# A cached-attention decode block on one core: TensorE's tail moved 820 instructions on, one load cut by rows, one by columns

## The chip, the cores and the metric

One core of one Trainium2 chip. The metric is the device time of one execution in microseconds (us); several runs are taken and their median counts. The profile is of one more execution, whose own time stands beside its span.

## What is computed

A decode step of a transformer block, batch 2, one new position, model width 448, all in fp32:

```python
h  = x + _A_ref(_layernorm(x), k_cache, v_cache, wq, wo)   # 16 heads of 256, 8192 cached keys
h2 = h + _B_ref(_layernorm(h), w_gate, w_up, w_down)       # ((h Wg) * (h Wu)) Wd, width 1792
```

`_A_ref` projects q, takes scores against the cached keys (scaled by 256^-0.5), a softmax over the 8192 keys, mixes the cached values and projects by wo. Keys and values are 2 x 16 x 8192 x 256 floats each: of the 561 MB that are read, 537 MB are these two caches.

## The kernel before

The work is 32 attention items, one for each head and batch row (`NQ = H * B`), and then the output projection and the gated feed-forward layer. Keys of item i, [128 partitions, 64 positions, 256], land in one of two buffers `k0`, `k1`; values in the one buffer `v`. VectorE multiplies the keys by the spread query (L436) and sums over the 256 (L445), all in place; TensorE and ScalarE make the softmax from the scores, and TensorE mixes the values (`mix`, L527). Once the last keys are used, weights take the place of keys and values: wo in `k0`; gate and up in `k1`; down in `v`.

**Queues.** All loads but x's are issued by SyncE (SP), in the order of the list that `load` (L175) builds, each by one `dma_start` (its line in the profile is L176). At the end of that list come wo, the last values in two parts, gate's weights (L283), up's weights in three loads by columns (L284, `wu0` to `wu2`: 3584, 1792 and 896 columns), and down's weights in six (L287, `DOWN`: 4, 4, 2, 2, 1 and 1 of the 14 chunks of 448 columns). Up's loads have no wait of their own; down's wait for the last mix, `("M", NQ - 1)`. Every load has 128 rows, one a partition. x's load (L259) has two rows and is issued by ScalarE. Gate, up and down are packed on the host so that a partition's share of a load is one contiguous row.

**Engines.** `Engine.do` adds an instruction with its waits and its mark to a list for each engine; `Engine.emit` (L81) writes the list out when the program is built. `roll` (L59) makes a loop of it: TensorE's 32 turns (`tensor_turn`, L591) are one loop (L627), with parts for the last turn alone (`only`). What stands behind L627 is TensorE's last part: `last_head` (L577), the sums of the second layernorm, `project` for gate and for up (L710; matmuls at L715 and L726), the transposes of the product (L760), and down's matmuls (L779 for the first 8 chunks, L805 for the other six, four column quarters q each). One fp32 matmul is two weight loads and two passes on TensorE, so that counts in the profile are twice those in the code.

**Hints.** Before an engine's list, `emit` writes a branch that is never taken to a block `aside` at the end of the engine's code, and a hint for the target of the branch in `aside` (L90 to L97):

```python
hint = e.mark_branch_hint_location()
e.reg_mov(never, 0)
e.br_lt(never, 0, on_true=name + "aside", on_false=name + "main")
```

**Matmuls that are not read.** `busy(n)` (L534) puts four matmuls of n columns, eight passes, into a bank that nobody reads any more. They stand in the last turn (384), at L631 (256), L633 (320), L748 (384, between gate's and up's projection), L750 (256) and L773 (192).

**The end.** Each of down's matmuls waits for the load of its chunk, `("wd", down_of[k])` (L809). After the last, VectorE copies y out of PSUM (L815) and SP stores it (L818).

## Time and profile before

| | |
|---|---|
| median of 3 runs | 1301.18 us (1301.15 to 1301.63) |
| the profiled execution | 1300.94 us, span 1299.6 us (1.34 us lie outside the span) |
| busy | DVE 1132.5 us (87%), PE 471.1 (36%), PEld 149.9, ACT 83.5, POOL 0.8 |
| DMA | 561.28 MB, 432 GB/s over the span, 11382 packets |
| chain that ended last | DMA 48%, DVE 41%, issue 8%, PE 2% |

A span runs from the first to the last instruction of the program. The busy line tells how long each engine worked at all; the chain tells which work followed on which, back from the end. A DMA share is the mean over the core's 16 DMA engines: 1.00 when all 16 move data throughout a stretch (in a short stretch it can come out above 1, since a packet counts from its start). PE's matmuls are pipelined, so its rows overlap a little.

### The profile page before, as it was taken

How to read it: one execution, taken by the hardware profiler on the slowest of the kernel's cores; microseconds unless marked ns; L12 is line 12 of the kernel's file. 1: busy time of each engine (PE TensorE's matmuls, PEld its weight loads, DVE VectorE, ACT ScalarE, POOL GpSimd, SP SyncE). 2: the span in 40 equal slices, each digit the busy share in tenths (PEclk: the TensorE clock that was granted, in tenths of full speed). 3: DMA queues.
4: the chain of work that ended last, by engine and by line, in shares of the span. 5: the costliest groups of instructions: out<-in, count | busy, mean ns of one | idle time of the engine just before them, and what ended most of it. 6: DMA issues, size and time to landing. Idle time of an engine off the chain costs nothing.

```text
span 1299.6 us, 7381 instructions
## 1 busy us (share of the span) xinstructions
PE 471.1 (36%) x2870; PEld 149.9 (12%) x2870; DVE 1132.5 (87%) x265; ACT 83.5 (6%) x245; POOL 0.8 (0%) x8
## 2 busy tenths in 40 slices
PE   3643214334323433323334322433322343332368
PEld 0111001101001101101101101101100110100113
DVE  1999988889888889888889988889988888988861
ACT  1100000000000000000000000000000000000000
POOL 0000000000000000000000000000000000000000
PEclk9866566666566666556666656666656666655669
DMA  9999999999999999999999999999999999999998
GB/s 412 428 450 422 448 424 444 426 436 436 422 450 422 450 422 448 424 444 426 436 436 422 450 422 450 422 448 424 444 426 436 436 422 450 422 450 422 448 422 365
DMA packets 11382, 561.28 MB, mean 432 GB/s; under 512 B 1394, under 2 KB 1652, under 8 KB 2420
## 3 DMA queue, kind: packets, MB, share of 16 engines
q1 hardware_dynamic: 11376, 561.25, 99.8%
q8 instruction: 2, 0.03, 0.0%
q10 hardware_dynamic: 4, 0.00, 0.0%
HBM read 561.19 MB, written 0.06 MB: 432 GB/s over the span
## 4 chain that ended last, share of the span: by engine, by line
DMA 48%; DVE 41%; issue 8%; PE 2%; SPq 0%; DVEq 0%; ACT 0%
DMA k<-in_A_k_cache_dram 45%; DVE s L445 21%; DVE k L436 19%; DMA v<-in_wq_dram 2%; DMA v<-in_wd_dram 1%; PE bank L376 1%; PE bank L561 1%; PE bank L527 1%; DVE m L458 0%; DVE nm L464 0%; DVE rl L469 0%; SPq L176 0%; PE bank L551 0%; DVEq L149 0%; PE bank L367 0%
## 5 line engine op out<-in xcount | busy, mean ns | idle before, releaser
L436 DVE TENSOR_TENSOR k<-k,qb 128x4096 f32<-128x4096 f32 x64 | 555.3, 8676 | 122.6 <-DMA k<-in_A_k_cache_dram 98.9
L445 DVE TENSOR_REDUCE s<-k 128x16 f32<-128x4096 f32 x64 | 555.2, 8675 | 1.1
L527 PE MATMUL bank<-v,p 128*2 128x512 f32 x2048 | 289.5, 729 | 348.0 <-DMA v<-in_A_v_cache_dram 348.0
L527 PEld LDWEIGHTS bank<-v,p 128*2 128x2 f32 x2048 | 53.2, 96 | 577.2 <-DMA v<-in_A_v_cache_dram 370.7
L597 PE MATMUL bank<-nm,row 1*128 1x1 f32 x64 | 18.6, 357 | 230.9 <-DVE nm L464 230.9
L594 PE MATMUL bank<-ident,m 128*1 128x128 f32 x32 | 11.9, 372 | 179.7 <-DVE m L458 179.7
L502 ACT ACTIVATE o_sb<-bank 128x512 f32<-128x512 f32 x32 | 19.1, 597 | 625.9 <-PE bank L527 625.9
L597 PEld LDWEIGHTS bank<-nm,row 1*128 1x128 f32 x64 | 15.9, 306 | 240.3 <-DVE nm L464 240.3
L619 PE MATMUL bank<-sel,o_sb 128*128 128x1 f32 x256 | 33.7, 253 | 22.6 <-ACT o_sb L502 22.6
L367 PE MATMUL bank<-q_sel,ones 2*128 2x256 f32 x68 | 40.2, 691 | 0.0
L619 PEld LDWEIGHTS bank<-sel,o_sb 128*128 128x128 f32 x256 | 31.0, 191 | 52.3 <-ACT o_sb L502 52.3
L376 PE MATMUL bank<-v,xz 128*2 x64 | 30.5, 639 | 16.3 <-DMA v<-in_wq_dram 16.3
L492 ACT ACTIVATE nb<-bank 128x1 f32<-128x1 f32 x32 | 5.5, 171 | 427.0 <-PE bank L597 427.0
L601 PE MATMUL bank<-lsum,ones 128*128 128x1 f32 x64 | 18.7, 361 | 23.5 <-ACT p L494 23.5
L594 PEld LDWEIGHTS bank<-ident,m 128*1 128x1 f32 x32 | 2.5, 79 | 182.7 <-DVE m L458 182.7
L601 PEld LDWEIGHTS bank<-lsum,ones 128*128 128x128 f32 x64 | 16.0, 309 | 26.2 <-ACT p L494 26.2
L404 ACT ACTIVATE q_sel<-q_all,ident 2x256 f32 (+1 forms) x35 | 17.2, 492 | 0.0
L413 ACT ACTIVATE qb<-bank 128x256 f32<-128x256 f32 x34 | 13.0, 383 | 58.2 <-PE bank L367 58.2
L367 PEld LDWEIGHTS bank<-q_sel,ones 2*128 2x128 f32 x68 | 16.4, 297 | 2.2 <-issue 1.7
L494 ACT ACTIVATE p<-s,nb 128x64 f32<-128x64 f32 x32 | 11.1, 348 | 1.0
L504 ACT ACTIVATE oT<-bank,rl 128x2 f32 x32 | 8.4, 262 | 42.0 <-PE bank L619 42.0
L487 DVE COPY k<-bank 128x448 f32<-128x448 f32 x1 | 0.6, 624 | 11.6 <-PE bank L561 11.6
(89 smaller groups left out, 96.0 us busy)
## 6 DMA issues: line engine op xcount, KB each, us to landing
v<-in_wq_dram SPq DMA_DIRECT2D x1, 7168.0 KB, 19.7
k<-in_wo_dram SPq DMA_DIRECT2D x1, 7168.0 KB, 39.6
k<-in_A_k_cache_dram SPq DMA_DIRECT2D x1, 6144.0 KB, 38.1
v<-in_A_v_cache_dram SPq DMA_DIRECT2D x1, 6144.0 KB, 22.8
k<-in_wg_dram SPq DMA_DIRECT2D x1, 3136.0 KB, 27.8
k<-in_A_k_cache_dram SPq DMA_DIRECT2D x1, 2048.0 KB, 24.1
v<-in_A_v_cache_dram SPq DMA_DIRECT2D x1, 2048.0 KB, 27.3
k<-in_wu_dram SPq DMA_DIRECT2D x1, 1792.0 KB, 31.8
```

Source lines behind the costliest of these rows:

```text
L367: lambda *_: nc.tensor.matmul(qb_ps, ones[:B, :], q_sel, start=True, stop=True),
L376: lambda turn, k=k, c=c, xs=xs, base=base: nc.tensor.matmul(q_ps[k], xz[:, xs, :], wq_t[:, bass.ds(turn * QG + base, QG)], start=(c == 0), ...
L404: return nc.scalar.activation(q_sel, q_sb[:, bass.ds(at, DH)], AF.Copy, scale=ident[:B, b : b + 1])
L413: lambda *_: nc.scalar.activation(qb[i % 2], qb_ps, AF.Copy),
L436: lambda *_: nc.vector.tensor_mul(kt, kt, q[:, None, :].to_broadcast([P, hi - lo, DH])),
L445: lambda *_: nc.vector.tensor_reduce(s[:, lo:hi], kt, axis=AX.X, op=ALU.add),
L502: A.do(lambda *_: nc.scalar.activation(o_sb, o_ps, AF.Copy), ("M", i), done=("osb", i))
L527: lambda *_, t=t, g=g: nc.tensor.matmul(o_ps[g : g + 2, :], p_t[:, 2 * t : 2 * t + 2], v_sb[:, 2 * t : 2 * t + 2, :], start=(t < 4), stop= ...
L594: lambda *_: nc.tensor.transpose(mT_ps, m_t, ident), ("m", i), done=("T", i)
L597: lambda *_: nc.tensor.matmul(nb_ps, row, nm, start=True, stop=True),
L601: lambda *_: nc.tensor.matmul(l_ps, ones, lsum, start=True, stop=True),
L619: lambda *_, c=c, k=k: nc.tensor.matmul(oT_ps[:, c : c + 1], o_sb[:, (2 * k + c) * P : (2 * k + c + 1) * P], sel[:, k : k + 1], start=(k = ...
```

## The change

Four edits. (1) Behind TensorE's loop a branch skips 820 instructions that are never run (1640 waits, two to an instruction) to a block `far`, which holds TensorE's last part; a hint for `far` is given at the start of TensorE's program, and the hint for `aside` is now given at the start of `far`. (2) The first quarter of `wu0` (`F // 2`, 896 columns, which is 3584 bytes a row) is loaded ahead by two loads, of rows 0 to 103 and of rows 104 to 127, onto the semaphore of `wu0`, which now counts 48; the rest of `wu0` (2688 columns) follows. (3) `busy(384)` between the two projections is left out. (4) The last chunk of down's weights comes in two loads of 224 columns each; the matmuls of its last two quarters wait for the second one.

```diff
+APART, EVEN = 820, 104
@@ Engine.__init__
-        self.items, self.ahead, self.gap = [], 0, None
+        self.items, self.ahead, self.gap, self.far, self.apart_by = [], 0, None, None, 0
@@ Engine.emit
         self.emit_ops(self.items[: self.ahead], known, seen)
+        at = self.ahead
+        if self.far is not None:
+            hint = e.mark_branch_hint_location()
+            e.reg_mov(never, 0)
+            self.emit_ops(self.items[at : self.far], known, seen)
+            e.br_lt(never, 0, on_true=name + "unused", on_false=name + "far").branch_hint(hint)
+            with nc.body(name + "unused", valid_engines=here):
+                for _ in range(2 * self.apart_by):
+                    e.wait_ge(self.sems[0], 0)
+                nc.br(name + "far", engines=here)
+            nc.switch_bb(name + "far")
+            at = self.far
         hint = e.mark_branch_hint_location()
...
-            self.emit_ops(self.items[self.ahead : self.gap], known, seen)
+            self.emit_ops(self.items[at : self.gap], known, seen)
@@ decode_block, the loads
-    for k, part in enumerate((slice(0, 2 * F), slice(2 * F, 3 * F), slice(3 * F, NF * D))):
-        load(S, wu_t[:, part], wu[:, part], landing(f"wu{k}"), ("wu", k))
+    wu_ends, s_wu = (2 * F, 3 * F, NF * D), [landing(f"wu{k}") for k in range(3)]
+    for rows in (slice(0, EVEN), slice(EVEN, P)):
+        load(S, wu_t[rows, : F // 2], wu[rows, : F // 2], s_wu[0], "wu_even")
+    for k, part in enumerate(map(slice, (F // 2, *wu_ends), wu_ends)):
+        load(S, wu_t[:, part], wu[:, part], s_wu[k], ("wu", k), n=16 * (3 if k == 0 else 1))
     at = 0
     for k, n in enumerate(DOWN):
-        load(
-            S, v_flat[:, at * D : (at + n) * D], wd[:, at * D : (at + n) * D],
-            landing(f"wd{k}"), ("wd", k), ("M", NQ - 1),
-        )
+        mid = [at * D + 2 * W] if k == len(DOWN) - 1 else []
+        ends = [at * D, *mid, (at + n) * D]
+        for j, cols in enumerate(map(slice, ends, ends[1:])):
+            load(
+                S, v_flat[:, cols], wd[:, cols], landing(f"wd{k + j}"), ("wd", k + j),
+                ("M", NQ - 1),
+            )
         at += n
@@ decode_block, TensorE
     T.roll(0, NQ, 1, tensor_turn)
+    T.far, T.apart_by = len(T.items), APART
...
-    busy(384)
     project(u_ps, wu_t, lambda c: ("wu", max(c - 1, 0)), "u", "u_blank")
...
-                ("hmT_in", j // 2), ("wd", down_of[k]),
+                ("hmT_in", j // 2), ("wd", down_of[k] + (k == NF - 1 and q >= 2)),
```

## Rows read from the trace of the kernel before

**Rows 1.** page, the DMA line of part 2, and part 3 (queue, kind: packets, MB, share)

```profile
DMA  9999999999999999999999999999999999999998
...
q1 hardware_dynamic: 11376, 561.25, 99.8%
q8 instruction: 2, 0.03, 0.0%
q10 hardware_dynamic: 4, 0.00, 0.0%
```

**Rows 2.** chain of work that ended last, in order of time, from 1276 us (start, us, what)

```profile
1276.97 0.33 SPq L176
...
1279.31 17.89 DMA v<-in_wd_dram
...
1297.24 0.44 PE bank L805 x8
...
1297.71 0.27 DVE k L815
```

**Rows 3.** stretches near the end (us, granted TensorE clock, DMA share of 16 engines, GB/s)

```profile
1295.40:1295.80 0.40, 1.00 0.38 143
1295.80:1296.00 0.20, 1.00 0.18 72
1296.05:1296.25 0.20, 1.00 0.12 45
1296.60:1296.85 0.25, 1.00 0.13 50
1296.90:1297.20 0.30, 1.00 0.00 0
```

**Rows 4.** DMA queues, instruction fetch: first 60 to 80 us, then 1282 to 1284.5 us

```profile
q8 instruction: 1, 0.02, 0.3%
...
q8 instruction: 1, 0.02, 2.4%
```

**Rows 5.** DMA queues and issues, 1298 to 1299.6 us (engine, KB each, us to landing)

```profile
q1 hardware_dynamic: 144, 0.06, 12.9%
...
out_dram<-k SPq DMA_DIRECT2D x1, 56.0 KB, 1.5
```

**Rows 6.** page, part 6: two of the loads (KB each, us from issue to landing)

```profile
k<-in_wg_dram SPq DMA_DIRECT2D x1, 3136.0 KB, 27.8
...
k<-in_wu_dram SPq DMA_DIRECT2D x1, 1792.0 KB, 31.8
```

**Rows 7.** timeline (start, us, engine line op tiles shape count [idle before])

```profile
1238.42 8.54 PE L527 MATMUL bank<-v,p 128*2 128x512 f32 x64 [11.61 <-DMA v<-in_A_v_cache_dram]
...
1254.63 1.37 SPq L176 DMA_DIRECT2D k<-in_wu_dram  x3
...
1269.86 7.05 PE L527 MATMUL bank<-v,p 128*2 128x512 f32 x64
...
1277.63 1.05 PE L619 MATMUL bank<-sel,o_sb 128*128 128x1 f32 x8
...
1278.61 0.61 PE L539 MATMUL bank<-k,sel 128*2 128x256 f32 x8
...
1286.82 0.83 PE L539 MATMUL bank<-k,sel 128*2 128x384 f32 x8
...
1287.46 2.74 PE L715 MATMUL bank<-k,xr 128*32 128x512 f32 x24
...
1293.93 0.93 PE L779 MATMUL bank<-v,k 128*2 128x448 f32 x8 [0.23 <-DMA v<-in_wd_dram]
...
1295.15 0.59 PE L805 MATMUL bank<-v,k 128*32 128x112 f32 x16 [0.29 <-DMA v<-in_wd_dram]
...
1297.24 0.40 PE L805 MATMUL bank<-v,k 128*32 128x112 f32 x8 [0.16 <-DMA v<-in_wd_dram]
```

**Rows 8.** a stretch before the last but one item's mix (us, PE busy, granted clock, DMA, GB/s)

```profile
1225.50:1238.00 12.50, 1.32 (x3) 0.50 0.95 410
```

## The prediction

> **What bounds the kernel now.** The page comes first. Its DMA line is at 9 tenths or more in 39 of 40 slices and 8 in the last, and the packets of q1 fill 99.8% of 16 engines' span [rows 1]. 561.25 MB over 0.998 x 16 x 1299.6 us is 27.0 KB per us and engine. The compute engines work beside that: the DMA queue is never empty, so the kernel ends when the last of the 16 engines has worked off its share, plus what follows that.

> The chain in order of time shows what follows. SP issues the last of the down loads at 1279.31, it has landed 17.89 us later, at 1297.20; then 0.44 us of eight matmul passes of L805, the copy (0.27), and the store, 1299.6 being the span's end [rows 2]. So 2.4 us lie behind the last landing.

> Third, the last microseconds in short stretches [rows 3]. The reader is to see steps of 1/16 = 0.0625 in the DMA share: 0.38 on average up to 1295.8, then 0.18 (three engines), 0.12 and 0.13 (two), and 0 from 1296.90. Thirteen engines are done by 1295.8, a third straggler between 1296.00 and 1296.05 (1296.04 in what follows), and two work on alone for 0.9 us. The landing at 1297.20 is 0.30 after their last packet.

> Why two? The other entry that moves bytes is the fetch of instructions, 2 packets in the whole span [rows 1]. One falls between 60 and 80 us and took 0.3% of 16 x 20 us, about 1.0; one between 1282 and 1284.5, 2.4% of 16 x 2.5, or 0.96 us, of one engine [rows 4]. An engine that served one is that much late with its loads, and since its queue never empties it stays late. Two fetches, two engines late by 0.9: I read them as cause and effect, though no row numbers the engines.

> **The change, part by part.**

> [...]

> Cutting rows costs packets: 144 packets of the store took 12.9% of 16 x 1.6 us, 23 ns each, of which 448 bytes are 17 ns, so 6 ns more for each. An engine of the twelve gets 10 more packets here, 8 with the cut down chunk, and three marks: about 0.12 us, a spared engine 0.06.

> *The last down chunk in two loads.* The second half waits alone at the end, so four passes instead of eight stand behind the last landing. The eight took 0.40 [rows 7]; four save 0.2. The added wait delays nothing but the last two quarters of y; the first two run earlier.

> *SP.* Two more issues for up, one more for down, at 1.37/3 = 0.46 us [rows 7]. Up's were issued 31.8 us before the first landed [rows 6], down's last 17.89 before; SP's next work is the store. Nothing at the end; without that cover, 1.4 us.

> *The unread matmuls* (eight passes of 384 columns): 1286.82 to the next start at 1287.46, 0.64 us of TensorE [rows 7]. Up's projection follows at once, since its first load, issued at 1254.63, landed 31.8 later, 1286.4 [rows 6]; at the end it gives nothing, as TensorE waits for down's loads at 1293.93, 1295.15 and 1297.24 [rows 7]. No idle time appears there, so the clock should stay at 1.00 [rows 3].

> *TensorE's jump.* A hint at the program's start lies in the wait for wq. After the last turn come a branch over 820 instructions, a hint and a second branch. The rows don't show such sequencer work. Cover: between L619's start at 1277.63 and the next matmul at 1278.61, 1.0 us [rows 7], the sequencer has only to run ahead. Lower bound 0 (no gain: nothing at this place holds the end); upper bound, if the code isn't there, a fetch of 0.96 behind one row of gate's weights (3136 KB over 128 rows, 24.5 KiB, 0.93 us [rows 6]), 1.9. I take 0, as neither fetch of now leaves a visible stall. The fetches themselves don't go away: each still costs one engine 0.96, and longer code may add one.

> *Sum.* If the late engines are spared ones: 1296.90 - 1.06 + 0.06 = 1295.90, no longer last. The thirteen go to 1295.8 + 0.27 + 0.12 = 1296.2, the third straggler to 1296.04 + 0.39 = 1296.43. That one now sets the end: landing at 1296.73, 0.47 earlier; with 0.2 from the four passes, 0.67. The profiled execution took 1300.94 (span 1299.6 and 1.34 around it), 0.24 under the median of 1301.18. I predict 1301.18 - 0.67 = 1300.5.

> **Rivals.**

> A, relief misses: a late engine is one of the twelve. 1296.90 + 0.39 = 1297.29, then 0.2 saved: +0.2, 1301.4; where the late engine is the one that neither gains nor loses, about 1301.1. For it: three of 16 are spared and no row names them. Against: the fetches, never on one engine twice here, seem to take engines in turn, and three spared neighbours cover a turn of up to three.

> B, more relief: the third straggler is spared as well, the end falls to 1296.2, 1300.3.

> C, the loads spread over all 16: -0.2 alone and a few marks, 1301.0. The hint doing nothing belongs to D.

> D, slower: the jump finds its code missing. Place: the branch after the last turn. Price: 1.9 less a cover of 0 to 1.0, so TensorE's tail is 0.9 to 1.9 late. [...] It decides beyond TensorE's slack: 0.64 of unread matmuls and idle 0.23, 0.29 and 0.16 [rows 7], 1.3 against the present end, 0.6 against the forecast. Alone: 1300.8 to 1301.8; with the clock, up to 1303.3; a second missing block, 1.9 more, 1304 to 1305. For it: two fetches in 1300 us show that the code isn't all loaded ahead [rows 1, 4]; against: the hint, given long before, and that neither fetch of now held TensorE, whose clock stays at 1.00 behind the second [rows 3].

> [...]

> **How the numbers follow.** 0.2% of 1301.18 is 2.6 us, about what a measurement of this kernel can tell from no change; all cases but D's far end lie inside. Chances: forecast 0.5, B 0.1, A 0.17, C 0.05, D up to 1301.8 0.08, D beyond 0.07 (past 2.6 us 0.03), unforeseen gain 0.03. The range holds the first five less their edges: from B with 0.4 of run-to-run spread, 1299.9, to A and D's near end, 1301.8. The forecast's own range, with 0.2 of spread and the marks, is 1300.2 to 1300.8. Faster by over 0.2%: 0.01, as no term reaches 2.6; slower 0.03; same 0.96.

> **What would show it.** Right: q1 near 11376 + 117 + 36 + 144 = 11673 packets (11680 if all loads had 16 marks); the DMA share drops to zero at about 1296.4 with no pair working on alone; the last landing at 1296.7; four passes of L805 behind it; L539 gone from before up's projection; no gap between L619 and the next matmul. Wrong: a pair alone to 1297.2 (A), the steps of now unchanged (C), a gap of over a microsecond behind L619 or a clock under 1.00 after 1278 (D), or more than three fetch packets on the engines.

## The result, and the profile after

The changed kernel takes 1303.76 us (median of 22 runs, 1301.62 to 1304.40), the kernel before, run beside it, 1301.18 (1300.96 to 1301.73). The ratio is 1.0018, with a 95% interval of 1.0012 to 1.0023: 2.6 us slower, where 1300.5 was predicted, in a range up to 1301.8. The profiled execution took 1303.55 us (span 1302.2), 2.61 more than that of before.

The page after, the lines that answer to [rows 1]:

```profile
DMA  9999999999999999999999999999999999999998
...
q1 hardware_dynamic: 11673, 561.25, 99.7%
q8 instruction: 2, 0.03, 0.0%
q10 hardware_dynamic: 4, 0.00, 0.0%
```

Same bytes, and 11673 packets as forecast, which fits 104 rows on 13 engines and 24 on 12 (117 and 36 packets with the end marks). The queue is as full as before, and there are still two instruction fetches. The chain after, in order of time (start, us, what), against [rows 2]:

```profile
1278.39 20.25 DMA v<-in_wd_dram
1298.64 0.04 issue
1298.68 1.56 PE bank L829 x32
1300.25 0.02 issue
1300.27 0.28 DVE k L839
```

The load still holds the end. The chain puts all 32 passes of L829 into one piece; the last four of them waited once more, for the last load, which landed at 1299.79:

```profile
1299.84 0.14 PEld L829 LDWEIGHTS bank<-v,k 128*32 128x32 f32 x4 [0.17 <-DMA v<-in_wd_dram]
```

y's copy (L839) starts at 1300.27, not 1297.71: 2.56 later. So the loss is all ahead of it. TensorE's timeline after (start, us, engine line operation, idle before and its releaser in brackets):

```profile
1277.73 1.05 PE L643 MATMUL bank<-sel,o_sb 128*128 128x1 f32 x8
...
1278.71 0.61 PE L563 MATMUL bank<-k,sel 128*2 128x256 f32 x8
...
1283.76 1.91 PE L740 MATMUL bank<-k,xr 128*32 128x512 f32 x16 [0.87 <-DMA k<-in_wg_dram]
...
1289.04 1.91 PE L740 MATMUL bank<-k,xr 128*32 128x512 f32 x16 [1.07 <-DMA k<-in_wu_dram]
...
1296.51 0.93 PE L803 MATMUL bank<-v,k 128*2 128x448 f32 x8 [0.71 <-DMA v<-in_wd_dram]
```

The jump lies between L643 and L563: 0.98 from start to start, as in [rows 7]. The first new wait is for gate's weights, behind which the cut quarter of up lies in the queue; before, gate's matmuls started without one:

```profile
1282.68 1.91 PE L715 MATMUL bank<-k,xr 128*32 128x512 f32 x16
```

So the next view is the DMA's rate while that quarter is loaded (us, granted TensorE clock, DMA share, GB/s), first before, then after:

```profile
1280.20:1280.70 0.50, 1.00 0.95 402
...
1280.80:1283.20 2.40, 1.00 1.04 441
1283.20:1286.20 3.00, 1.00 0.96 401
```

```profile
1280.20:1280.70 0.50, 1.00 0.71 287
1280.70:1281.20 0.50, 1.00 1.35 351
1281.20:1281.70 0.50, 1.00 0.98 244
1281.70:1282.20 0.50, 1.00 1.14 237
1282.20:1282.70 0.50, 1.00 1.37 272
...
1280.80:1283.20 2.40, 1.00 1.06 242
1283.20:1286.20 3.00, 1.00 1.00 370
```

This is the reading that counts: the share stays at 1, but 242 GB/s are moved in place of 441. The engines are as busy, their packets take longer. From 1280.8 to 1286.2 that is 2.4 x 199 + 3.0 x 31 = 571 KB less, 1.3 us at 432 GB/s. And at the very end, against [rows 3]:

```profile
1297.20:1297.50 0.30, 1.00 0.28 99
1297.70:1298.30 0.60, 1.00 0.13 48
1298.50:1299.40 0.90, 1.00 0.07 24
```

Two engines still work on alone, and then one (0.07) by itself up to 1299.49. To see what became of that one I followed single packets of the trace, each one starting where the last one on its engine ended. A last gate row (25088 bytes) and what came behind it, on the engine that ends last:

```
                      last gate row       then, until the first 3584 columns of up are in
kernel before   931 ns, ends 1281.755     8 rows of 14336 bytes, end 1286.01: 4.26 us
kernel after   1733 ns, ends 1282.676     8 rows, mark, 2 rows of 3584 bytes, mark,
                                          8 rows of 10752 bytes, end 1288.55: 5.88 us
```

So this engine had 8 + 2 rows: it is one of the twelve, not one of the three that were spared. Those ten packets of 3584 bytes took 141 to 348 ns, 237 in the mean; down's packets of that size, later in the same trace, took 140. It lost 0.92 us in the gate row's end and 1.62 behind it, 2.54 in all; the last landing came 2.59 later (1299.79 for 1297.20).

### The profile page after: what moved, and what is told of

It is laid out like the page before. It is cut to its first block, busy times and chain, and to the rows that moved or that the text cites. A ratio compares the mean times of both kernels' runs of the same rounds, so it can differ in the third digit from the quotient of the medians.

```text
span 1302.2 us, 7371 instructions
## 1 busy us (share of the span) xinstructions
PE 472.4 (36%) x2862; PEld 149.6 (11%) x2862; DVE 1132.5 (87%) x265; ACT 83.5 (6%) x245; POOL 0.8 (0%) x8
## 3 DMA queue, kind: packets, MB, share of 16 engines
q1 hardware_dynamic: 11673, 561.25, 99.7%
## 4 chain that ended last, share of the span: by engine, by line
DMA 74%; PE 25%; issue 0%; SPq 0%; DVE 0%
DMA v<-in_A_v_cache_dram 71%; PE bank L551 23%; PE bank L400 2%; DMA v<-in_wd_dram 2%; DMA v<-in_wq_dram 2%; PE bank L829 0%; SPq L193 0%; PE bank L391 0%; DVE k L839 0%
## 5 line engine op out<-in xcount | busy, mean ns | idle before, releaser
L643 PE MATMUL bank<-sel,o_sb 128*128 128x1 f32 x256 | 33.7, 253 | 22.6 <-ACT o_sb L526 22.6
L643 PEld LDWEIGHTS bank<-sel,o_sb 128*128 128x128 f32 x256 | 31.0, 191 | 52.3 <-ACT o_sb L526 52.3
```

The lines of the kernel that those rows point to most:

```text
L643: lambda *_, c=c, k=k: nc.tensor.matmul(oT_ps[:, c : c + 1], o_sb[:, (2 * k + c) * P : (2 * k + c + 1) * P], sel[:, k : k + 1], start=(k = ...
```

## The experiments

Each was run in turn with the kernel before. The letters in the expectations: T, the load by rows is slow in itself (P: because of the partitions that its engines write at one time); J, the jump costs; Q, the number of loads in the queue; U, the unequal shares of rows; R, the number and size of row loads, whichever rows they hold; F, the fetches go with the length of the code.

**Without the cut by rows, and the cut alone.** The first is the changed kernel with up's loads as before, the second the kernel before with edit 2 alone.

```diff
-    wu_ends, s_wu = (2 * F, 3 * F, NF * D), [landing(f"wu{k}") for k in range(3)]
-    for rows in (slice(0, EVEN), slice(EVEN, P)):
-        load(S, wu_t[rows, : F // 2], wu[rows, : F // 2], s_wu[0], "wu_even")
...
+    for k, part in enumerate((slice(0, 2 * F), slice(2 * F, 3 * F), slice(3 * F, NF * D))):
+        load(S, wu_t[:, part], wu[:, part], landing(f"wu{k}"), ("wu", k))
```

> The changed kernel with wu0 loaded in one load of 128 rows as before; the jump, the missing unread matmuls and the down chunk in two loads stay. Theory T: the two loads of 104 and 24 rows make engines write to the same group of SBUF partitions and halve the rate while they run (changed kernel: 244, 237 and 272 GB/s in half microseconds from 1281.2 to 1282.7, where before had 430 to 459), which costs every engine over 1 us. Then all of the loss goes: 1301.0, 0.2 under before by the four passes, and 430 GB/s in that stretch. Rival J: the jump over 820 instructions (with the later fetch of code) is the loss: stays at 1303.7. Rival Q: the longer list of loads on SP (the last load was issued 5 us late, at 1284.58) is the loss: half back at most, 1302.5, since one more load than before is left.

> The kernel before with only the first quarter of wu0 as 104 and 24 rows. T: slower by the whole loss and by the four passes that the changed kernel saves, 1303.9, with the same dip to some 240 GB/s. J: 1301.2, no loss. Q: two more loads than before against three in the changed kernel, about 1302.9.

Without the cut: 1301.27 us, ratio 0.9999 (0.9990 to 1.0008). The cut alone: 1303.71, ratio 1.0016 (1.0007 to 1.0025). The whole loss is edit 2; the other three together are worth nothing that shows. The same two stretches, without the cut, and with the cut alone:

```profile
1280.80:1283.20 2.40, 1.00 0.98 412
1283.20:1286.20 3.00, 1.00 0.99 418
```

```profile
1280.80:1283.20 2.40, 1.00 1.13 261
1283.20:1286.20 3.00, 1.00 0.96 346
```

The dip goes with the cut, and J falls. In the second trace the engine that ends last shows the same two things: its last gate row took 1616 ns, and 8 + 2 rows of 3584 bytes follow. The first also has edit 4, whose end shows in its timeline:

```profile
1297.63 0.14 PEld L826 LDWEIGHTS bank<-v,k 128*32 128x32 f32 x4 [0.16 <-DMA v<-in_wd_dram]
1298.06 0.27 DVE L836 COPY k<-bank 128x112 f32<-128x112 f32 x1 [2.12 <-PE bank L826]
```

The four passes behind the last landing start at 1297.63, and the copy 0.43 later; before, with eight passes, 0.47 [rows 2]. So half as many of them save 0.04, not 0.2.

**The quarter whole, and cut at 64.** The changed kernel with the quarter ahead in one load of 128 rows; and with `EVEN = 64`, where both halves run on all 16 engines (q1 has 11680 packets, 80 for each half) and none is spared. In the runs with another number of loads the count of `wu0`'s semaphore follows that number.

```diff
-    for rows in (slice(0, EVEN), slice(EVEN, P)):
+    for rows in (slice(0, P),):
...
```

> The changed kernel with the first quarter of wu0 in one load of 128 rows, ahead of the rest: the columns are still cut, the rows are not. T: no dip, 1301.0 to 1301.1 (eight more packets of 6 ns an engine). Q or a cost of short rows (3584 bytes): one load fewer than in the changed kernel, 1302.5 to 1303. J: 1303.7.

> The changed kernel with the quarter cut at row 64 instead of 104: two loads of 64 rows, 64 being divisible by 16, so that no engine is spared and each has 4 rows of either. [...] Rival U: the loss comes from sparing three engines (they run ahead and out of step) or from two more rows on the twelve others: no dip, 1301.1.

Whole: 1301.57, ratio 1.0001 (0.9992 to 1.0010). Cut at 64: 1303.04, ratio 1.0013 (1.0004 to 1.0022). In the same order:

```profile
1280.80:1283.20 2.40, 1.00 1.06 431
```

```profile
1280.80:1283.20 2.40, 1.00 1.06 277
1283.20:1286.20 3.00, 1.00 0.99 370
```

So a smaller load ahead, of rows as short as those of the cut, costs nothing that the interval can tell. Q falls: this kernel issues as many loads as the one with the cut alone, which took 2.1 us more. And a cut that gives all engines equal shares still loses 1.7 of the 2.6 us, so U is not the main cause; it may hold a part of the rest. T's sizes were off: the whole quarter came out 0.3 us above no change, which its interval can't tell from it, and the cut at 64 cost 1.5 on top, where half the rate for its 448 KB would cost 1.06 (an estimate, 448 KiB / 432 GB/s).

**Same sizes, other rows.** Three loads of 64, 32 and 32 rows, first with rows 32 to 95 as the 64, then with rows 0 to 63.

```diff
-    for rows in (slice(0, EVEN), slice(EVEN, P)):
+    for rows in (slice(32, 96), slice(0, 32), slice(96, P)):
...
```

```diff
-    for rows in (slice(0, EVEN), slice(EVEN, P)):
+    for rows in (slice(0, 64), slice(64, 96), slice(96, P)):
...
```

> The changed kernel with the quarter in three loads: rows 32 to 95 (64 rows), then 0 to 31, then 96 to 127. [...] Loss 0.5 us against the same without a row cut, 1301.6 plus 0.3, 1301.9, against the kernel of the next run, with the same sizes, 0.5 less; no dip in its first half microsecond. Rival R: any cut by rows costs alike (short loads, rows out of step): as the next run.

> The changed kernel with the quarter in three loads of the same sizes but rows 0 to 63, 64 to 95, 96 to 127. [...] R: no difference between the two.

Rows 32 to 95: 1301.78, ratio 1.0003 (0.9994 to 1.0012). Rows 0 to 63: 1303.14, ratio 1.0014 (1.0005 to 1.0023). In the same order:

```profile
1280.80:1283.20 2.40, 1.00 1.10 379
1283.20:1286.20 3.00, 1.00 0.96 397
```

```profile
1280.80:1283.20 2.40, 1.00 1.03 264
1283.20:1286.20 3.00, 1.00 1.01 394
```

Number and size of the loads and the packets (11696) are the same; only the rows differ, by 1.36 us and 115 GB/s. R falls: it matters which rows a load holds. A row is both a partition and a row of the source in memory, and no run moves one without the other; that the partitions are what counts is argued, since the 64 source rows lie at the same distances in both runs. The late engine's last gate row, which it is still moving while the others are at the cut load, is a plain gauge: 931 ns in the kernel before and with the quarter whole, 1156 with rows 32 to 95, 1627 with rows 0 to 63, 1536 at 64, and 1733 after. Another is the time that the packets of the 128 cut rows themselves took:

```
                       mean ns   rows at 142 ns or less
quarter whole              140   128
rows 32 to 95 first        147   110
rows 0 to 63 first         196    52
cut at 64                  199    50
changed kernel             208    42
```

The 0.5 us that this cut was expected to lose with rows 32 to 95 first is about what both loads of 32 rows cost at half rate (an estimate: 224 KiB / 432 GB/s = 0.53). No run shows it: with rows 32 to 95 first, 110 rows kept the full rate (142 ns or less), so at least 46 of the 64 rows in those two loads, and the loss against the whole quarter is 0.2 us.

**The cut on twice as many columns.** 104 and 24 rows of 1792 columns.

```diff
-        load(S, wu_t[rows, : F // 2], wu[rows, : F // 2], s_wu[0], "wu_even")
-    for k, part in enumerate(map(slice, (F // 2, *wu_ends), wu_ends)):
+        load(S, wu_t[rows, :F], wu[rows, :F], s_wu[0], "wu_even")
+    for k, part in enumerate(map(slice, (F, *wu_ends), wu_ends)):
```

> The changed kernel with twice the columns (the first half of wu0, 1792 columns, 7168 bytes a row) loaded as 104 and 24 rows. T and P: the dip to half rate lasts twice as long, so the loss of 2.4 us becomes about 4.8: 1306.0. If three spared engines were what mattered and their relief merely fell short, twice the relief (2.1 us) would bring gain: under 1303.7. If the loss is a fixed cost of loads that use 13 and 12 engines (start and end of a load): 1303.8.

1306.06 us, ratio 1.0034 (1.0024 to 1.0044), and the dip lasts about twice as long:

```profile
1280.80:1283.20 2.40, 1.00 1.02 231
1283.20:1286.20 3.00, 1.00 1.03 184
```

The relief that was meant would have doubled as well. The price goes with the bytes that are loaded by rows: 4.8 us for 896 KB, 2.6 for 448 KB. A fixed cost of such loads, 1303.8, falls with that.

**The other edits, and the fetches.** The kernel before without the three sets of unread matmuls behind the attention (L748, L750, L773); with the jump alone (edit 1); with the last chunk's two loads alone (edit 4).

```diff
-    busy(384)
...
-    busy(256)
...
-    busy(192)
```

```diff
...
     T.roll(0, NQ, 1, tensor_turn)
+    T.far, T.apart_by = len(T.items), APART
```

```diff
+        mid = [at * D + 2 * W] if k == len(DOWN) - 1 else []
+        ends = [at * D, *mid, (at + n) * D]
...
-                ("hmT_in", j // 2), ("wd", down_of[k]),
+                ("hmT_in", j // 2), ("wd", down_of[k] + (k == NF - 1 and q >= 2)),
```

> The kernel before without the unread matmuls of L748, L750 and L773: 48 instructions less on TensorE, 738 in place of 786. [...] Then one fetch packet in the whole span, one engine alone in the last 0.9 us in place of two, and hardly any gain, 1301.1, as the other is still late; unless the clock falls without them. Rival: the lateness has another cause (the place of the rows): two engines alone as before.

> The kernel before with edit 1 alone: TensorE's last part 820 instructions on, hinted. T (all the loss is the load by rows): as before, 1301.2, between 1300.9 and 1301.6; gap between the start of the last turn's last row of sums and the next matmul 1.0 us; two fetches. If the jump costs or gains on its own account: over 1301.6 or under 1300.9. If the number of fetches sets the number of late engines and this program has three fetches, three engines work on alone at the end.

> The kernel before with edit 4 alone: the last down chunk in two loads by columns. T: as before within 0.2 us, 1301.1 to 1301.3, with four passes behind the last landing and the copy's start 0.48 us behind that landing, as in no_row_split. If the saving of 0.2 us is there but was hidden in no_row_split by another edit: 1301.0, the copy 0.3 us behind the landing.

They took 1301.31 (ratio 1.0001, 0.9992 to 1.0010), 1301.34 (1.0001, 0.9992 to 1.0010) and 1301.63 us (1.0002, 0.9993 to 1.0011). None differs from the kernel before; the last lies above its expected span, and no gain of 0.2 shows. F missed, and no run shows a fetch that goes with these instructions: with 48 matmul passes and weight loads fewer on TensorE there were still two fetches, and two engines alone at the end of the kernel without unread matmuls:

```profile
1295.40:1295.80 0.40, 1.00 0.46 170
...
1296.05:1296.25 0.20, 1.00 0.12 45
1296.60:1296.85 0.25, 1.00 0.11 43
1296.90:1297.20 0.30, 1.00 0.00 0
```

The jump's timeline shows once more no cost of the branch, 0.98 from start to start:

```profile
1277.77 1.05 PE L636 MATMUL bank<-sel,o_sb 128*128 128x1 f32 x8
...
1278.75 0.61 PE L556 MATMUL bank<-k,sel 128*2 128x256 f32 x8
```

Whether a fetch makes an engine late can be read without another kernel. Each load leaves 16 end marks, one an engine. The latest four, in us behind the median of the 16:

```
kernel before (fetches start at 77.51 and 1282.95)
first mark at 58.25     0.15  0.16  0.32  0.62
first mark at 77.59     0.13  0.28  0.62  1.69
gate, from 1280.49      0.19  0.27  0.56  1.38
up, from 1284.74        0.24  0.52  1.36  1.41
last of down, 1295.63   0.23  0.52  1.27  1.34
jump alone (fetches start at 77.65 and 1281.51)
gate, from 1280.57      0.15  0.17  0.50  1.42
up, from 1284.82        0.12  0.50  1.41  1.46
```

One engine falls back by a microsecond in the load that spans the first fetch, and a second one in the load that spans the other. Both stay late to the end.

## Why the prediction was wrong

**The step that failed** is "Up's first quarter as 104 and 24 rows". It bounded how the rows are shared, at one end over all 16 engines and at the other eight rows each on 13, and took the second, which was right: 11673 packets. But it priced each row at 0.133 us in both cases, "3584 bytes a row, 0.133 us at 27.0 KB per us", a rate that only loads of 128 rows show in the trace. For a load of another number of rows there was no row, so that this price needed a bound of its own on the high side; only 0.12 us of extra packets was added. On the engine that ends last a row took 0.237 us in the mean, and over all 128 rows 0.208. That the other engines' rows slow down an engine that is still at gate's weights was no term at all, and that alone was 0.8 us (1733 for 931 ns).

**"If the late engines are spared ones"** failed too: in the two traces that I followed, the engine that ends last has 8 + 2 rows. Nor was the engine spared that served the second fetch, at 1283.38 in the trace after: its first row of 10752 bytes starts at 1281.85, behind an end mark, where three engines start theirs at 1280.46, 1280.52 and 1281.04. That is rival A's condition, to which I gave 0.17. Its price, 1301.4, was 2.4 us short, since it kept the same rate.

By its own account the late engine's 2.54 us are 0.92 up to the end of its gate row; two more rows at 140 ns, 0.28 where 0.27 was forecast; and 1.34, the rest, which holds the 0.12 that was forecast for more packets and otherwise rows that took longer beside the others. Three engines were ahead of the rest at the end, as they should: the first three marks of the last load stand at 1296.55 to 1296.97, the bulk at 1297.37 to 1297.59. But spared engines don't help one that isn't spared.

Could a better cut have relieved it? I found none, and none of these kernels beats the one before. Every partition must still get its bytes, and that other engines can fill a late engine's partitions faster isn't shown: from 1280.8 to 1283.2 the kernels with a cut by rows moved 231 to 277 GB/s, 379 with rows 32 to 95 first, and the kernel before 441.

**Step by step.** What bounds the kernel: right, the load holds the end in every run. Two fetches as two late engines: right by the end marks. The four passes: 0.2 forecast, 0.04 measured, since most of [rows 7]'s 0.40 for eight doesn't go with their number (0.47 to the copy for eight, 0.43 for four). The added issues on SP: nothing, as said; though SP was held at the last of them (see below). The unread matmuls: nothing, as said. The jump: 0, as taken, and D's condition did not come: there is no gap (0.98 from start to start, as before). The lower clock, which makes D's 1303.3, is a term that no run shows at this place: the granted clock stays at 1.00 in the stretches shown above. Past 1301.8 only D had a chance, 0.07; the slower result came by a mechanism that no rival held. And 2.6 us, taken as about the least that a measurement can tell, was told well: the interval is some 0.7 us to either side.

**Open.** Two of the 22 runs of the changed kernel took 1301.62 and 1301.83, and two runs each of the cut alone (1301.62, 1302.11) and of the cut on twice the columns (1303.56, 1304.09) also came out lower than the rest; what spared them isn't known. Half the rate for 448 KB would add 448 KiB / 432 GB/s = 1.06 us, and the cut costs 2.4 alone and 2.6 in the changed kernel. The account of the late engine says where the rest lies: it is held up in its own gate row and again among the cut rows. Why the hold-up fell so unevenly on the engines isn't shown, nor why loads of 32 rows kept the full rate. How the rows of a cut load fall to partitions and engines was not seen in a trace, only the rates.

## What to carry to other kernels

When an edit changes the shape of a transfer, not only its size, price its rate anew: a rate seen on loads of 128 rows (140 ns a row) didn't hold here for loads of 104 and 24 (208), or of 64 (199). Look at GB/s beside the busy share: here a share of 1.06 at 242 GB/s, where the kernel before moved 441 at 1.04, was packets that took longer, not more bytes moved. And before a load is shared out to relieve a late engine, find out which engine is late: its end marks and the packets that follow them tell.

## What was unexpected

A far branch over 820 instructions cost TensorE nothing visible (0.98 us from start to start with it and without), and no third fetch came with it: 2 packets of q8 in every kernel. Whether the hint or the wait between the two matmuls covered it isn't shown, as no run leaves the hint out. The second fetch took 960 to 964 ns on its engine in the six kernels without a cut by rows, and 1140 to 1369 in the six with one (961 before, 1194 after). And SP was held by its last issues: the sixth and seventh down load took it 5.2 and 2.7 us after the change, where the others took 0.33 to 0.43, and the seven together 10.22 us, where six took 3.27 before. Nothing waited for them. With seven down loads and no cut by rows it was 6.98 us (all edits but the cut). SP's timeline of the changed kernel, and of the kernel before:

```profile
1277.07 10.22 SPq L193 DMA_DIRECT2D v<-in_wd_dram  x7
```

```profile
1276.97 3.27 SPq L176 DMA_DIRECT2D v<-in_wd_dram  x6
```
